# Windowed and pooled attention ahead of a gated feed-forward: from pair 12 on, every attention matmul becomes a 64x64 tile

## Chip, cores and metric

One Trainium2 chip, one of its cores. The metric is the device time in microseconds (us) of one execution, median of several; lower is better.

## The reference

Eight batches, eight heads, 576 positions, head dimension 64. Each head's attention is the sum of two parts. The first averages q, k and v over groups of four positions, attends among the 144 averages and repeats each result four times. The second lets every position see the positions less than four away. The result, as 4608 tokens by 512, goes through a feed-forward layer whose gate is a ReLU.

```python
q_d = q.reshape(B, H, Sd, factor, D).mean(axis=3)      # factor 4, Sd = 144; k_d, v_d alike
out_d = sm_attn(q_d, k_d, v_d)
out_up = np.repeat(out_d, factor, axis=2)
mask = np.abs(pos[:, None] - pos[None, :]) < factor
scores = np.where(mask, scale * np.matmul(q, k.transpose(0, 1, 3, 2)), -1e9)
out_local = np.matmul(softmax(scores), v)
x = (out_up + out_local).transpose(0, 2, 1, 3).reshape(B * S, H * D)
return (np.maximum(x @ w_gate, 0.0) * (x @ w_val)) @ w_out   # 512 -> 1536 -> 512
```

## The kernel before

**Pairs and chunks.** Two heads make a pair: head 0 lies on partitions 0 to 63, head 1 on 64 to 127. There are 32 pairs, four to a batch. The feed-forward works on chunks of 512 tokens, nine in all, each in two units of 256 tokens. Its result x, transposed, is the tile `xT`; `emit_h_mm` (L638) multiplies it with `w_gate` and `w_val`, ACT takes the ReLU (L647), DVE the product (L650), and the second product with `w_out` is done by a seven-product scheme on 128x256 quarters (`Unit.mm`, L723), whose sums are formed by DVE (L717). The last chunks use the same scheme for the first product too (L910).

**Order.** The schedule is by hand: the program emits each engine's instructions in the order of three token lists. `FRONT` covers pairs 0 to 11, `ORDER` is one period of four pairs and one chunk and is run for pairs 12 to 31, `TAIL` is what is left. A token is kind/argument/unit; within a period pairs a and b of units 0 and 1 follow each other. Each engine works through its own instructions in order.

**One pair's attention.** POOL issues the loads of q and k, cast to fp16 (L308), of v (`emit_load_v`, L333: 112 rows for each block of 96 queries, as the window reaches three further on either side) and of v grouped by four (`emit_load_v4`, L338). SP transposes q and k into `qkT` by DMA (L343); DVE sums groups of four into `qkd` (L350). POOL sums v by four in two steps (`emit_v2`, L385, and `emit_v1`, L391) into `vd`.

- `scores` (`emit_s1_mm`): pooled scores, four matmuls of 144 columns with 64 x 72 weights (L426); then for each of six blocks of 96 queries and both heads a matmul with 64 x 128 weights and 96 columns (L437). The two heads lie on the two row halves of PE. PSUM banks 4 to 7.
- `exp` (L447, twice) and `ed` (L461) on ACT, `mask` (L453, twice) on DVE.
- `o` (`emit_s2w_mm`), four times: three matmuls of 96 columns (L584) and two of 72 (L592) with weights 128 wide. Next to a head's 64 columns of v lie 64 columns of ones, so one matmul gives numerators on one half of the partitions and denominators on the other.
- `ln` (L602, twice, 64 partitions each) and `inv` (L607) on ACT give one over the denominator; `xn` (L611, twice, 64 partitions each) on DVE multiplies; `xsum` (L570) adds the pooled part, repeated four times, and writes `xT`.

Pairs 4 to 7 have another form, with denominators from a matmul with ones (`emit_den`, L527 and L536) and numerators apart (`emit_num`, L548 and L557), all 64 columns wide, so that the two heads lie on the two column halves. Pairs 8 to 11 have the `o` form, within `FRONT`.

**The start.** DVE sets tiles to constants, PE runs matmuls on a tile of zeros (`zero_sb`, L811), POOL issues the first loads of k and v. SP loads the first q and the constants and later issues the transposes and the output writes (L673), in the order of the program.

Of the kernel before, what the change touches and what calls it, by code (L numbers as in the profile page):

```python
# [106 lines left out]
"""  # L107
LATE = ("gate/5/1", "gate/4/1", "next/0/1", "next/1/1")
ORDER = """
p/1/0 gate/5/1< scores/a/0 keep/1/0 gate/4/1< hg/0/0 exp/a0/0 sumhi/0/0 sumhi/1/0 exp/a1/0  # L110
hv/0/0 mask/a0/0 ed/a/0 mask/a1/0 p/2/0 next/0/1< relu/0/0 next/1/1< o/a00/0 o/a01/0 c11//0
o/a10/0 ln/a0/0 o/a11/0 sum/2/0 p/6/0 v/a/1 sum/3/0 p/5/0 keep/2/0 pool/b/0 v2/b/0 ln/a1/0 p/7/0
hg/2/0 keep/3/0 after/3/0 v1/a/1 inv/a/0 c22//0 p/4/0 gate/0/0 v2/a/0 p/3/0 xn/a1/0 c21//0 relu/2/0 hg/1/0
xn/a0/0 qk/a0/1 hv/2/0 relu/1/0 qk/a1/1 c12//0 xsum/a/0 scores/b/0 qk/a2/1 next/0/0 hv/1/0
exp/b0/0 v/b/0 exp/b1/0 hg/4/0 mask/b0/0 gate/1/0 v4/a/1 ed/b/0 hg/3/0 mask/b1/0 relu/4/0
gate/2/0 v1/b/0 o/b00/0 o/b01/0 o/b10/0 pool/a/0 ln/b0/0 o/b11/0 hv/4/0 v2/a/1 ln/b1/0 hv/3/0
gate/4/0 inv/b/0 v4/b/1 next/1/0 p/1/1 relu/3/0 xn/b1/0 v4/b/0 p/2/1 keep/1/1 qk/a3/1 hg/5/0
xn/b0/0 qk/b0/1 p/6/1 gate/3/0 relu/5/0 qk/b1/1 scores/a/1 next/2/0 keep/2/1 next/3/0 hg/0/1
v/b/1 exp/a1/1 exp/a0/1 hv/5/0 mask/a1/1 qk/b2/1 ed/a/1 mask/a0/1 p/7/1 qk/b3/1 c11//1 gate/5/0
o/a00/1 keep/3/1 o/a01/1 o/a10/1 pool/b/1 ln/a0/1 o/a11/1 p/5/1 qk/a0/0> ln/a1/1 p/4/1 v/a/0>  # L120
c22//1 inv/a/1 hv/0/1 xsum/b/0 qk/a1/0> c21//1 xn/a0/1 p/3/1 relu/0/1 v2/b/1 hg/1/1 xn/a1/1
hg/2/1 relu/1/1 qk/a2/0> xsum/a/1 scores/b/1 c12//1 qk/a3/0> relu/2/1 gate/0/1 hg/3/1 exp/b1/1
v4/a/0> exp/b0/1 hv/1/1 mask/b1/1 ed/b/1 mask/b0/1 hv/2/1 gate/1/1 relu/3/1 pool/a/1 o/b00/1
o/b01/1 o/b10/1 ln/b0/1 o/b11/1 hv/3/1 qk/b0/0> gate/2/1 ln/b1/1 qk/b1/0> hg/5/1 gate/3/1
inv/b/1 v1/a/0> hv/4/1 relu/5/1 xn/b0/1 v1/b/1 hg/4/1 qk/b2/0> xn/b1/1 hv/5/1 relu/4/1 qk/b3/0>
xsum/b/1
"""


def _np_constants():  # L130
    i = np.arange(128)[:, None]
    p = np.arange(96)[None, :]
    band = ((i - p >= 0) & (i - p <= 6)).astype(np.float16)
    m_first = band * (i >= 3)
    m_last = band * (i <= 98)
    masks = np.stack([m_first, band, band, m_last], axis=1)
    pool = np.zeros((128, 176), np.float16)
    rw = np.arange(3, 99)
    pool[rw, 48 + (rw - 3) // 4] = 1.0
    t96 = np.arange(96)[:, None]  # L140
    eye = (t96 == np.arange(96)[None, :]).astype(np.float16)
    sum4 = (t96 // 4 == np.arange(24)[None, :]).astype(np.float16)
    t72 = np.arange(72)[:, None]
    rep4 = (t72 == np.arange(288)[None, :] // 4).astype(np.float16)
    cst = np.zeros((128, 384 + 176 + 120 + 288), np.float16)
    cst[:, 0:384] = masks.reshape(128, 384)
    cst[:, 384:560] = pool
    cst[:96, 560:656] = eye
    cst[:96, 656:680] = sum4
    cst[:72, 680:968] = rep4  # L150
    return cst


# [15 lines left out]
def kernel(  # L169
# [24 lines left out]
    LEAD = 4  # L194
    NTP = 9
    NVP = 11
    VS = 7
    NK = NJJ // 2
    B0 = 1
    WK = 112  # L200
# [5 lines left out]
    small = ctx.enter_context(tc.tile_pool(name="small", bufs=4))  # L206
    ypool = ctx.enter_context(tc.tile_pool(name="ypool", bufs=4))

    zero_sb = keep.tile([128, 640], FP16, name="zero_sb")
    cst_sb = keep.tile([128, 968], FP16, name="cst_sb")  # L210
    masks_sb = cst_sb[:, 0:384]
    pool_sb = cst_sb[:, 384:560]
    eye_sb = cst_sb[0:96, 560:656]
# [6 lines left out]
    def ring(n, shape, dtype, name):  # L220
        return [keep.tile(shape, dtype, name=f"{name}{i}") for i in range(n)]
# [3 lines left out]
    PS = 8  # L225
    qkfull = ring(NL, [128, 2, 2 * NB * 64], FP16, "qk16_")
    qk16 = [t[0:96] for t in qkfull]
    v4 = ring(NV4, [72, 4, 256], FP16, "v4_")
    v2full = ring(2, [128, 4, 128], FP32, "v2_")
    v2 = [t[0:72] for t in v2full]  # L230
    vwfull = ring(NL, [128, 2 * NB, 128], FP16, "vw_")
    vw = [t[0:WK] for t in vwfull]
    qkT = ring(4, [128, 2 * S + 32], FP16, "qkT_")
    qkd = ring(2, [128, 2, SD], FP16, "qkd_")
    ee = ring(2, [WK, 2, S + 32], FP16, "ee_")
    ed = ring(2, [72, 2, 2 * SD + 64], FP16, "ed_")
    vd = ring(3, [72, 2, 192], FP16, "vd_")
    xofull = keep.tile([128, 3, NB + 2, 128], FP16, name="xo")
    xo = [xofull[0:96, i] for i in range(3)]
    rden = keep.tile([128, 2, 360], FP32, name="rden")  # L240
# [4 lines left out]
    q32 = q32full[0:96]  # L245
    r1 = ring(3, [128, TCH], FP16, "r1_")
    gT = ring(2, [128, NJJ, TCH], FP16, "gT_")
    xT = keep.tile([128, NPB, NTOK], FP16, name="xT")
    ps = psum.tile([128, 8, 512], FP32, name="ps")

# [19 lines left out]
    nc.vector.memset(zero_sb, 0.0)  # L270
    nc.vector.memset(ones_sb[:, 0:64], 1.0)
    nc.vector.memset(ones_sb[:, 64:128], 4.0)
    for t in vw[0:4]:
        nc.vector.memset(t[:, :, 64:128], 1.0)
    for t in qkT:
# [15 lines left out]
    def head_off(hp):  # L291
        b = (hp // NPB + B0) % B
        return b, (b * H + 2 * (hp % NPB)) * S * D
# [17 lines left out]
        )  # L311

    def emit_load_v(hp):
        r = hp % NL
        b, off = head_off(hp)
        base = off - 3 * D
        t = vw[r][:, :, 0:64]
        n = 2 * NB
        if off == 0:
            nc.gpsimd.dma_start(  # L320
                t[:, 1:, :], _dap(v, base + NQ * D, [[D, WK], [NQ * D, n - 1], [1, D]])
            )
            nc.gpsimd.dma_start(t[3:WK, 0, :], _dap(v, 0, [[D, WK - 3], [1, D]]))
            nc.gpsimd.dma_start(t[0:3, 0, :], _dap(v, 0, [[D, 3], [1, D]]))
        elif b == B - 1 and hp % NPB == NPB - 1:
            nc.gpsimd.dma_start(
                t[:, 0 : n - 1, :], _dap(v, base, [[D, WK], [NQ * D, n - 1], [1, D]])
            )
            last = base + (n - 1) * NQ * D
            nc.gpsimd.dma_start(t[0:99, n - 1, :], _dap(v, last, [[D, 99], [1, D]]))  # L330
            nc.gpsimd.dma_start(t[99:WK, n - 1, :], _dap(v, last, [[D, WK - 99], [1, D]]))
        else:
            nc.gpsimd.dma_start(t, _dap(v, base, [[D, WK], [NQ * D, n], [1, D]]))  # L333

    def emit_load_v4(hp):
        b, off = head_off(hp)
        if hp >= NVP:
            nc.gpsimd.dma_start(  # L338
                v4[hp % NV4], _dap(v, off, [[4 * D, 72], [72 * 4 * D, 4], [1, 4 * D]])
            )  # L340

    def emit_qkT(hp):
        nc.sync.dma_start_transpose(  # L343
# [4 lines left out]
    def emit_pool(hp):  # L348
        with nc.allow_low_precision(reason="4:1 pooling sum"):
            nc.vector.tensor_reduce(  # L350
                out=qkd[hp % 2].rearrange("p i t -> p (i t)"),
                in_=qkT[hp % 4][:, 0 : 2 * S].rearrange("p (t f) -> p t f", f=4),
                axis=AX.X,
                op=ALU.add,
            )
# [14 lines left out]

    def emit_flipped(hp, i, pooled, eng, bank):
        if pooled:
            o = qkd[hp % 2].rearrange("p i t -> p (i t)").rearrange("p (b n t) -> p b n t", b=3, n=4)
        else:
            o = qkT[hp % 4][:, 0 : 2 * S].rearrange("p (b n t) -> p b n t", b=3, n=4)
        t = ps[:, bank, 0:480].rearrange("p (n t) -> p n t", n=4)
        copy_on(eng)(out=o[:, i], in_=t[:, :, 96:120] if pooled else t[:, :, 0:96])  # L377
# [2 lines left out]
        return nc.scalar.copy if eng == "A" else nc.vector.tensor_copy  # L380

    def emit_v2(hp):
        if NVP <= hp < NP:
            t, m = v4[hp % NV4], v2[hp % 2]
            nc.gpsimd.tensor_tensor(out=m, in0=t[:, :, 0:128], in1=t[:, :, 128:256], op=ALU.add)  # L385

    def emit_v1(hp):
        if not NVP <= hp < NP:
            return
        m, o = v2[hp % 2], vd[hp % 3]  # L390
        nc.gpsimd.tensor_tensor(  # L391
            out=o.rearrange("p c (x d) -> p x c d", x=3)[:, 0:3:2, :, :],
            in0=m[:, :, 0:64].rearrange("p (h c) d -> p h c d", h=2),
            in1=m[:, :, 64:128].rearrange("p (h c) d -> p h c d", h=2),
            op=ALU.add,
        )
# [180 lines left out]
    def emit_s2w_mm(hp, hh, g):  # L577
# [13 lines left out]
        for c in range(2):  # L591
# [4 lines left out]
                start=(c == 0),  # L596
                stop=(c == 1),
            )

    def emit_ln(hh):  # L600
        lo, de = 64 * hh, 64 - 64 * hh
# [406 lines left out]
    }  # L1008

    def scores(hp, a):  # L1010
        emit_s1_mm(hp, 4)
        if PS + 3 + LEAD <= hp + 3 < NP:
            emit_qkT(hp + 3)

# [3 lines left out]
    def pool_ab(hp, a):  # L1018
# [3 lines left out]

    PAIR_STEPS = {
        "scores": scores,
        "exp": lambda hp, a: emit_exp(hp, 4, int(a)),
        "mask": lambda hp, a: emit_mask(hp, int(a)),
        "ed": lambda hp, a: emit_ed(hp, 4),
        "o": lambda hp, a: emit_s2w_mm(hp, int(a[0]), int(a[1])),
        "ln": lambda hp, a: emit_ln(int(a)),
        "inv": lambda hp, a: emit_inv(),  # L1030
        "xn": lambda hp, a: emit_xnw(int(a)),
        "xsum": lambda hp, a: emit_xsum(hp),
        "pool": pool_ab,
        "v1": lambda hp, a: emit_v1(hp + 1),
        "v2": lambda hp, a: emit_v2(hp + 2),
# [66 lines left out]
    with tc.manual_schedule(engines={ET.PE, ET.DVE, ET.Activation, ET.SP, ET.Pool}):  # L1102
        nc.scalar.dma_start(cst_sb[0:96, 560:680], cst_dr[0:96, 560:680])
        emit_load_q1(0, 0)
        nc.sync.dma_start(cst_sb[:, 0:560], cst_dr[:, 0:560])
        nc.sync.dma_start(cst_sb[0:72, 680:968], cst_dr[0:72, 680:968])
        emit_warm(14, wide=True)
        for tok in FRONT.split():
            emit_front(tok)
# [37 lines left out]
```

## Time and profile before

| | |
|---|---|
| runs | 344.65, 345.5, 345.66 us; median 345.5 |
| profiled execution, first to last instruction | 343.5 us |
| what lies around the span (median less span) | 2.0 us |
| granted TensorE clock, mean | 0.998 |
| PE busy | 335.8 us (98%) |
| DVE, ACT, POOL busy | 295.2, 218.3, 181.9 us |
| L426 and L437, L584 and L592: matmuls | 128 and 384, 288 and 192 |

The profiled execution has no time of its own beside its span, so sums made from the trace are held against the span, and 2.0 us are added for the runs. Busy times of PE are modelled, and matmuls overlap: a row's mean for one matmul (203 ns for L437) is longer than the step from one to the next. What a stretch costs on PE is therefore read from the chain of work that ended last, in order of time, and from start times.

### The profile page before, as it was taken

To read this page: it belongs to the slowest core of one execution; us is meant where nothing else is said; L and a number is where in the kernel's file an instruction comes from. 1 tells how busy PE (TensorE), PEld (TensorE's weight loads), DVE (VectorE), ACT (ScalarE), POOL (GpSimd) and SP (SyncE) were. 2 spreads that over 40 slices of the span, in tenths; PEclk is the share of its full clock that TensorE was granted. 3 is DMA by queue.
4 is the path that set the end of the run, shared out by engine and by line. 5 is a ranking of instruction groups with operands and counts; after the bars stand their busy time and mean duration, and the time that the engine had idled before them with its cause. 6 is when DMAs were issued, how large, how long until landed. Compare 5 with 4: busy or idle time off the path is not lost.

```text
span 343.5 us, 8292 instructions
## 1 busy us (share of the span) xinstructions
PE 335.8 (98%) x3244; PEld 216.0 (63%) x3244; DVE 295.2 (86%) x546; ACT 218.3 (64%) x423; POOL 181.9 (53%) x232
## 2 busy tenths in 40 slices
PE   7899999999999999999999999999999999999996
PEld 3765556756575756575666656665766557768785
DVE  6695679988999999999999999999999798886892
ACT  3878766767767776676667767776677633334222
POOL 8986547776999893969297878740300000000000
PEclk9999999999999999999999999999999999999999
DMA  9999999999999999999989996991100001001023
GB/s 133 165 170 187 186 191 160 148 163 159 213 139 176 148 183 87 132 133 163 125 100 147 145 161 80 158 150 37 47 17 32 31 2 46 32 31 61 28 67 108
DMA packets 167882, 39.87 MB, mean 116 GB/s; under 512 B 149820, under 2 KB 164772, under 8 KB 167844
## 3 DMA queue, kind: packets, MB, share of 16 engines
q0 software_dynamic: 132160, 22.63, 92.1%
q1 hardware_dynamic: 35572, 16.71, 27.0%
q8 instruction: 25, 0.41, 0.5%
q14 instruction: 13, 0.11, 0.1%
q10 hardware_dynamic: 112, 0.02, 0.0%
HBM read 45.72 MB, written 9.44 MB: 161 GB/s over the span
## 4 chain that ended last, share of the span: by engine, by line
PE 90%; ACT 4%; DVE 3%; DMA 2%; issue 1%; POOL 0%; DVEq 0%; ACTq 0%; POOLq 0%
PE ps L638 48%; PE ps L723 23%; PE ps L910 4%; PE ps L584 4%; PE ps L437 2%; PE ps L426 2%; PE ps L592 2%; DMA vw<-in_v_dram 1%; PE ps L363 1%; PE ps L407 1%; DVE ee L453 1%; ACT qkT L377 1%; ACT ee L447 1%; ACT ed L461 1%; DVE xn L611 1%
## 5 line engine op out<-in xcount | busy, mean ns | idle before, releaser
L638 PE MATMUL ps<-xT,wv_sb 128*128 128x512 f16 x432 | 109.0, 379 | 0.0
L638 PE MATMUL ps<-xT,wg_sb 128*128 128x512 f16 x352 | 88.4, 380 | 0.0
L647 ACT ACTIVATE r<-ps 128x512 f16<-128x512 f32 x88 | 52.0, 596 | 31.6 <-PE ps L638 28.5
L638 PEld LDWEIGHTS <-wv_sb 128*128 128x128 f16 x432 | 40.4, 98 | 39.7
L650 DVE TENSOR_TENSOR gT<-r,ps 128x512 f16<-128x512 f16 x88 | 59.0, 680 | 6.7 <-PE ps L638 3.9
L638 PEld LDWEIGHTS <-wg_sb 128*128 128x128 f16 x352 | 32.6, 98 | 32.3 <-issue 0.2
L611 DVE TENSOR_TENSOR xn<-ps,rden 64x720 f16<-64x720 f32 x48 | 43.4, 905 | 5.3 <-ACT rden L607 4.1
L602 ACT ACTIVATE rden<-ps 64x720 f32<-64x720 f32 x48 | 36.7, 765 | 14.4 <-PE ps L592 13.3
L447 ACT ACTIVATE ee<-ps 112x576 f16<-112x576 f32 x64 | 38.8, 648 | 5.9 <-PE ps L437 4.9
L308 POOL DMA_DIRECT2D qk<-in_k_dram x46 | 33.9, 740 | 8.4 <-DMA qk<-in_q_dram 3.8
L308 POOL DMA_DIRECT2D qk<-in_q_dram x46 | 33.8, 740 | 6.9 <-DMA qk<-in_k_dram 1.7
L453 DVE TENSOR_TENSOR ee<-ee,cst_sb 112x576 f16<-112x576 f16 x64 | 32.3, 524 | 5.8 <-ACT ee L447 5.2
L723 PEld LDWEIGHTS <-gT 128*128 128x128 f16 x324 | 31.5, 98 | 9.0
L723 PEld LDWEIGHTS <-xo 128*128 128x128 f16 x288 | 27.4, 98 | 7.4
L333 POOL DMA_DIRECT2D vw<-in_v_dram x30 | 28.8, 960 | 5.8 <-PE ps L638 1.5
L350 DVE TENSOR_REDUCE qkd<-qkT 128x288 f16<-128x1152 f16 x23 | 30.9, 1344 | 0.0
L757 ACT COPY q<-ps 128x256 f32<-128x256 f32 x45 | 16.8, 373 | 21.1 <-PE ps L723 20.7
L723 PE MATMUL ps<-wo_sb,gT 128*128 128x256 f16 x216 | 28.0, 273 | 0.0
L723 PE MATMUL ps<-wt,xo 128*128 128x256 f16 x216 | 27.7, 272 | 0.0
L385 POOL TENSOR_TENSOR v<-v 72x512 f32<-72x512 f16 x21 | 24.8, 1182 | 3.7 <-DMA v<-in_v_dram 3.1
L920 ACT COPY vw<-ps 128x256 f32<-128x256 f32 x30 | 10.8, 374 | 20.7 <-PE ps L910 13.8
L570 DVE TENSOR_TENSOR xT<-xn 128x576 f16<-128x576 f16 x28 | 22.6, 808 | 0.5
(110 smaller groups left out, 556.9 us busy)
## 6 DMA issues: line engine op xcount, KB each, us to landing
out_dram<-y_sb SPq DMA_DIRECT2D x24, 256.0 KB, 4.0
vw<-in_v_dram POOLq DMA_DIRECT2D x30, 168.0 KB, 6.8
qk<-in_q_dram POOLq DMA_DIRECT2D x46, 72.0 KB, 6.6
qk<-in_k_dram POOLq DMA_DIRECT2D x46, 72.0 KB, 6.6
v<-in_v_dram POOLq DMA_DIRECT2D x21, 144.0 KB, 6.9
out_dram<-y_sb SPq DMA_DIRECT2D x22, 128.0 KB, 1.7
wg_sb<-in_moe_w_gate_dram POOLq DMA_DIRECT2D x4, 384.0 KB, 9.7
wv_sb<-in_moe_w_val_dram POOLq DMA_DIRECT2D x4, 384.0 KB, 10.5
```

The lines of the kernel that those rows point to most:

```text
L308: nc.gpsimd.dma_start(dst.rearrange("p (j h d) -> p j h d", h=2, d=64)[:, :, hh, :], _dap(src, off + hh * S * D, [[D, 96], [NQ * D, NB], [ ...
L333: nc.gpsimd.dma_start(t, _dap(v, base, [[D, WK], [NQ * D, n], [1, D]]))
L350: nc.vector.tensor_reduce(out=qkd[hp % 2].rearrange("p i t -> p (i t)"), in_=qkT[hp % 4][:, 0 : 2 * S].rearrange("p (t f) -> p t f", f=4), ...
L385: nc.gpsimd.tensor_tensor(out=m, in0=t[:, :, 0:128], in1=t[:, :, 128:256], op=ALU.add)
L447: nc.scalar.activation(out=o, in_=ps[0:WK, p0 + 2 * g : p0 + 2 * g + 2, 0:288], func=AF.Exp, scale=scale)
L453: nc.vector.tensor_tensor(out=o, in0=o, in1=_sap(masks_sb, (0, WK), 96 * g, [[0, 2], [1, 288]]), op=ALU.mult,)
L602: nc.scalar.activation(out=rden[lo : lo + 64], in_=ps[de : de + 64, 4 + 2 * hh : 6 + 2 * hh, 0:360], func=AF.Ln)
L611: nc.vector.tensor_tensor(out=xn[lo : lo + 64], in0=ps[lo : lo + 64, 4 + 2 * hh : 6 + 2 * hh, 0:360], in1=rden[lo : lo + 64], op=ALU.mult,)
L638: nc.tensor.matmul(out=out, lhsT=w[:, kk, bass.ts(jj, 128)], rhs=xT[:, kk, c * TCH : (c + 1) * TCH], start=(kk == 0), stop=(kk == 3),)
L647: nc.scalar.activation(out=r1[j % 3], in_=h1, func=AF.Relu)
L650: nc.vector.tensor_tensor(out=gT[c % 2][:, jj, :], in0=r1[j % 3], in1=h2, op=ALU.mult)
L723: nc.tensor.matmul(out=out, lhsT=left[:, i, :], rhs=right[i], start=(first and i == 0), stop=(i == NK - 1), skip_group_check=True,)
```

## The change

For pairs 12 to 31 the blocks of queries become 48 long. A block sees 54 keys, and 64 are taken. Even blocks lie on partitions 0 to 63 and odd ones on 64 to 127, for both heads, so that weights are 64 x 64 and four matmuls after one another go to four different quarters of PE.

- `emit_s1z`: pooled scores as 12 matmuls of 72 columns, windowed scores as 24 of 48; banks 4 and 5 only.
- `exp`, `mask` once for a pair, over 128 partitions x 576; `ed` 128 x 432.
- `den` (`emit_denz`): with ones as weights, 4 matmuls of 288 columns and 12 of 72 (three steps summed in PSUM), banks 6 and 7. `num` (`emit_numz`): 24 of 48 and 12 of 72, banks 4 and 5. On PE, `num` follows `den` with nothing between.
- `ln`, `xn` once for a pair, 128 x 720.
- v is loaded in two DMAs of 64 rows x 12 blocks (`emit_load_vz`). v by four is loaded in fp32 with two DMAs by SP instead of one with a cast by POOL; POOL's two sums work on 128 x 384 and 128 x 192; then two DMAs on SP copy the sums of each half of the partitions to the other, as both halves need both heads.
- Ahead of everything, POOL sets the three `v4` tiles (128 x 768 fp32) to zero; `near_sb`, the new mask, is one more load on SP; `zero_sb` is now part of `gT`.
- `ORDER` is the same list with the second tokens of `exp`, `mask`, `ln`, `xn` left out and the four `o` tokens replaced by `den` and `num`. `FRONT` and `TAIL` stay.

```diff
+    for t in v4:
+        nc.gpsimd.memset(t, 0.0)
...
     def emit_load_v4(hp):
+        if hp >= ZP:
+            t = v4[hp % NV4]
+            for h in range(2):
+                nc.sync.dma_start(
+                    t[64 * h : 64 * h + 48], _dap(v, off + h * S * D, [[4 * D, 48], [192 * D, 3], [1, 4 * D]])
+                )
...
+    def emit_load_vz(hp):
+        for par in range(2):
+            t = vz[hp % NL][64 * par : 64 * par + 64]
+            base = off + (48 * par - 3) * D
+                nc.gpsimd.dma_start(t, _dap(v, base, [[D, 64], [96 * D, 12], [1, D]]))
...
     def emit_v1(hp):
+        if hp >= ZP:
+            m, o = v2full[hp % 2], vdz[hp % 3]
+            nc.gpsimd.tensor_tensor(out=o[:, 0], in0=m[:, 0:3, 0:64], in1=m[:, 0:3, 64:128], op=ALU.add)
+            nc.sync.dma_start(o[64:112, 1], o[0:48, 0])
+            nc.sync.dma_start(o[0:48, 1], o[64:112, 0])
+            return
...
+    def emit_s1z(hp):
+        r4, f = hp % 4, qkdflat[hp % 2]
+        for c in range(3):
+            for g in range(2):
+                for h in range(2):
+                    rows, lo = slice(64 * h, 64 * h + 64), 288 + 72 * c
+                    nc.tensor.matmul(
+                        out=ps[64 * g : 64 * g + 64, 4 + h, lo : lo + 72].rearrange("p (j t) -> p j t", t=12),
+                        lhsT=f[rows, SD + 48 * c : SD + 48 * c + 64],
+                        rhs=f[rows, 0:SD].rearrange("p (j s t) -> p j s t", s=2, t=12)[:, :, g, :],
+                        start=True, stop=True)
+        t = qkT[r4]
+        for j in range(6):
+            for par in range(2):
+                for h in range(2):
+                    rows, lo = slice(64 * h, 64 * h + 64), 96 * j + 48 * par
+                    nc.tensor.matmul(
+                        out=ps[64 * par : 64 * par + 64, 4 + h, 48 * j : 48 * j + 48],
+                        lhsT=t[rows, S + lo - 3 : S + lo + 61],
+                        rhs=t[rows, lo : lo + 48],
+                        start=True, stop=True)
...
+    def emit_downz(hp, bank, left):
+        for c in range(3):
+            for g in range(2):
+                rows = slice(64 * g, 64 * g + 48)
+                for h in range(2):
+                    nc.tensor.matmul(
+                        out=ps[64 * h : 64 * h + 64, bank + g, 288:360],
+                        lhsT=left(rows, h ^ g, c),
+                        rhs=edfull[hp % 2][rows, h, 72 * c : 72 * c + 72],
+                        start=(c == 0), stop=(c == 2))
+
+    def emit_denz(hp):
+        for par in range(2):
+            rows = slice(64 * par, 64 * par + 64)
+            for h in range(2):
+                nc.tensor.matmul(
+                    out=ps[64 * h : 64 * h + 64, 6 + par, 0:288],
+                    lhsT=ones_sb[rows, 0:64],
+                    rhs=eefull[hp % 2][rows, h, 0:288],
+                    start=True, stop=True)
+        emit_downz(hp, 6, lambda rows, other, c: ones_sb[rows, 64:128])
+
+    def emit_numz(hp):
+        for j in range(6):
+            for par in range(2):
+                for h in range(2):
+                    nc.tensor.matmul(
+                        out=ps[64 * h : 64 * h + 64, 4 + par, 48 * j : 48 * j + 48],
+                        lhsT=t[rows, 6 * h + j, :],
+                        rhs=eefull[hp % 2][rows, h, 48 * j : 48 * j + 48],
+                        start=True, stop=True)
+        emit_downz(hp, 4, lambda rows, other, c: d[rows, other, c, :])
```

The first eighth of `ORDER`, after:

```
p/1/0 gate/5/1< scores/a/0 keep/1/0 gate/4/1< hg/0/0 exp/a/0 sumhi/0/0 sumhi/1/0 hv/0/0 mask/a/0
ed/a/0 p/2/0 next/0/1< relu/0/0 next/1/1< den/a/0 c11//0 ln/a/0 num/a/0 sum/2/0 p/6/0 v/a/1 sum/3/0
```

## Prediction

> **What bounds the kernel now.** I read the page first: the engines' shares and the chain that ended last.
>
> ```profile
> span 343.5 us, 8292 instructions
> ...
> PE 335.8 (98%) x3244; PEld 216.0 (63%) x3244; DVE 295.2 (86%) x546; ACT 218.3 (64%) x423; POOL 181.9 (53%) x232
> ...
> PE 90%; ACT 4%; DVE 3%; DMA 2%; issue 1%; POOL 0%; DVEq 0%; ACTq 0%; POOLq 0%
> ```
>
> PE is busy 98% and is 90% of the chain, so a change counts by what it does to PE's own stream; time taken off ACT and DVE counts only where PE waits for them. Next the chain in order of time (start, length, what) around one pair's attention:
>
> ```profile
> 67.72 2.59 PE ps L638 x12
> 70.31 0.18 PE ps L426 x2
> 70.49 0.13 PE ps L437 x6
> 70.62 0.06 PE ps L426 x2
> 70.68 0.13 PE ps L437 x6
> 70.81 2.70 PE ps L638 x12
> 73.50 0.13 PE ps L584 x3
> 73.64 0.07 PE ps L592 x2
> ```
>
> Two things are to be seen. The scores (L426, L437) are 0.50 us, and the twelve L638 matmuls behind them take 2.70 where the twelve before took 2.59. And one quarter of the outputs (L584, L592) is 0.20 us; the four quarters of a pair take 0.78 (64.76 to 65.54). The trace's start times say why. Matmuls 64 rows high on the two row halves start 3 ns apart and each such couple of 96 columns takes 42 ns, which is one matmul's streaming: they run side by side. Going from L638 to L426 costs 93 ns beyond the 216 ns that an L638 takes, and from L437 back to L638 92 ns beyond the 42; this repeats within 2 ns at every pair. I call these 0.185 us the price of one visit to small tiles. The outputs, full height and width, pay none. The pair's price on PE is 0.50 + 0.11 + 0.78 = 1.39 us.
>
> Side-by-side columns are shown by the first pairs, whose denominators and numerators are already 64 wide:
>
> ```profile
> 39.28 0.12 PE ps L527 x2
> 39.40 0.07 PE ps L536 x4
> 39.47 0.13 PE ps L548 x6
> ```
>
> Two 288-column matmuls in 0.12, four of 72 in 0.07: couples again, 0.033 us for 72 columns.
>
> Last, the start of the chain and the places where PE waits later:
>
> ```profile
> 0.64 0.66 issue
> 1.30 1.03 POOL qk L303
> 2.33 5.07 DMA vw<-in_v_dram
> ```
>
> ```profile
> 161.48 0.29 PE L584 MATMUL ps<-ee,vw 112*128 112x96 f16 x3 [0.35 <-DVE ee L453]
> ```
>
> The kernel starts with POOL issuing loads, and from pair 12 on one PE wait is worth naming: 0.51 us by start times before 161.48 (the other, 0.31 at 89.5, belongs to pair 11, which stays as it is).
>
> **PE, pairs 12 to 31 (20 pairs).** The new scores are 12 matmuls of 72 columns and 24 of 48, the denominators 4 of 288 and 12 of 72, the numerators 24 of 48 and 12 of 72, all on four 64x64 tiles in turn. If four run side by side, these are 3 + 6, 1 + 3 and 6 + 3 rounds. A 72-column round is 0.033 and a 288-column one 0.12 (rows above). No row has a 48-column round. From below: half of the 40 ns of a 96-column one and the same 2.5 ns beside it, 0.0225. From above: 0.033, since a 72-column round held its own 64-column weight loads. I take 0.028, near the shortest time from a 64-column weight load to its matmul in the start times (30 ns). Scores: 3 x 0.033 + 6 x 0.028 + one visit 0.185 = 0.45. Denominators and numerators follow each other on PE without a full-size matmul between, so they share one visit: 0.12 + 3 x 0.033 + 6 x 0.028 + 3 x 0.033 + 0.185 = 0.67. Sum 1.12 for 1.39: 0.27 less (0.20 to 0.33 by the two ends), times 20 is 5.4 us less (4.0 to 6.6).
>
> A rule is to be weighed here. The row: six L437 in 0.13 us, 22 ns each, couples 3 ns apart. The Trainium skill, TensorEngine Tiling (Array Packing), section Instruction Overhead, says that a matmul has about 60 cycles of overhead, that one column takes as long as 60, and that no tiling factor should come from a dimension that is already small; 48 columns are below it. Were that floor (25 ns, an estimate at the 2.4 GHz of its page on TensorE) paid by each instruction, the 88 matmuls would take 2.2 us and the time would be some 370 us, again an estimate; were it paid by each tile's round, the sum would gain 0.7 us. The row of couples speaks against the first reading.
>
> **ACT and DVE.** Rows of the costliest groups (busy us, mean ns, idle before):
>
> ```profile
> L611 DVE TENSOR_TENSOR xn<-ps,rden 64x720 f16<-64x720 f32 x48 | 43.4, 905 | 5.3 <-ACT rden L607 4.1
> L602 ACT ACTIVATE rden<-ps 64x720 f32<-64x720 f32 x48 | 36.7, 765 | 14.4 <-PE ps L592 13.3
> ```
>
> Each pair loses one of two exponentials (0.65), one Ln (0.77), one mask (0.52) and one product (0.91); ACT and DVE each lose 1.4 us per pair of about 9. PE covers all but the wait at 161.48: there the mask was late, it is now half the work, and I let 0.5 us go (0 to 0.5). Next late is nothing: between scores and denominators PE has two L638 groups and six L723, 2.4 us, for one exponential and one mask of 0.65 + 0.52.
>
> **The start.** Three POOL memsets of 128x768 fp32 now stand ahead of POOL's first load. The nearest row among POOL's groups:
>
> ```profile
> L1066 POOL MEMSET vw<- 112x768 f16 x3 | 2.5, 819 | 0.0
> ```
>
> It has as many elements per row in half the bytes; the instruction behind it starts 0.68 after it does. Three are 2.0 us from about 0.8 (DVE's first memset begins at 0.88), so the first load goes out near 2.9 to 3.1 instead of 1.30: 1.8 us late. From below 1.4 (the 0.66 of issue runs beneath them), from above 3.6 (twice the time for twice the bytes). The chain starts with just this load, and goes on through ACT and DVE without slack, so all of it is paid.
>
> **POOL, SP and DMA.** The v load becomes two issues (0.96 to about 2 x 0.8), the fp32 load (0.75) moves to SP, the two sums have fewer elements: POOL's total hardly moves. SP gains per pair two loads and two small copies that wait for POOL's sum; queued behind them are transposes and output writes. From pair 12 on the transposes go out 17 us or more before the pooling that reads them (73.5 and 90.4 for pair 12) and land in 7.8; POOL's sum ends 6 us or more before the matmul that reads it (92.9 and 98.9 for pair 12). The v loads have 1536 packets of 256 B for 1344, in a queue that runs as far ahead. I cost this at nothing; without that cover it is rival three.
>
> **Sum.** -5.4 - 0.5 + 1.8 = -4.1 us: span 339.4. The median of the runs (345.5) is 2.0 above the profiled span, so 341.4 us. The case's own ends: -6.6 - 0.5 + 1.4 and -4.0 + 3.6, 339.8 to 345.1.
>
> **Rivals.**
> *Only two tiles run at once* (slower). For it: no row shows row and column halves used together. Against: each alone runs as couples with nothing lost. Every round doubles: 2 x 0.756 + 0.37 = 1.88 per pair, +0.49 x 20 = +9.8; with the other terms 356.6 us. It decides from rounds 1.26 times my size on, where the 0.27 no longer pays for the start.
> *PE's sequencer can't feed it* (slower). 104 instructions, weight loads included, must pass in 0.49 us. The rows bound the rate from one side: after a semaphore wait at 19.60, 32 passed in 0.57 us, at most 18 ns each; the waits of L584 lie 0.45 to 1.2 us ahead of their matmuls, so the sequencer runs ahead. 104 x 18 ns less 1.0 of lead is 0.87, 0.38 more per pair, +7.6: 349.0 us. Should it be far faster, this is nothing.
> *SP's copies come late.* In pairs 14, 18, 22, 26 and 30 they go out behind a transpose (105.9 to about 113.7 for pair 14, needed at 117.1). A few us more of queueing stop PE; five stalls of 1 to 2 us, +7.5: 348.9 us.
> *Nothing is gained*: rounds at 0.033 and slow memsets leave it within 1 us.
>
> **How the numbers follow.** Forecast 0.60, two tiles 0.11, sequencer 0.10, copies 0.13, nothing 0.06. A measurement of this kernel can tell about 0.3%, 1.0 us. All of the forecast but its upper end (0.03) is faster: 0.57; same 0.09; slower 0.34. The range starts just below the forecast's own end and reaches up past the sequencer and the copies to 350; two tiles, and the far ends, stay out. The likeliest case alone is 339.8 to 345.1.
>
> **What would show it.** Right: scores in about 0.27 and denominators with numerators in about 0.49 us between full-size matmuls, four starts 3 ns apart, 93 ns at each change; no PE idle before either; first load near 3 us. Wrong: 48-column rounds at 0.05 or more (two tiles); matmuls that start singly 30 ns and more apart late in a burst (sequencer); PE idle released by vd or SP (copies); an L1066-like memset of 1.4 us (start).

## The result, and the profile after

The changed kernel takes 354.39 us (353.80 to 355.07); the kernel before, run beside it, 345.07. The ratio is 1.0265, with a 95% interval of 1.0232 to 1.0298. The forecast was 341.4 us, in a range from just below 339.8 to 350: wrong, and on the wrong side. The profiled execution, the shortest of the four, spans 351.9 us, 8.4 more than before. Times and ratios from here on leave out executions that took over 1.5% longer than the fastest of their kernel (one of the kernel without copies and early memsets, four of six with all sums on DVE, one of six with part of them there).

The page of the kernel after, its span, engines and chain:

```profile
span 351.9 us, 10404 instructions
...
PE 335.9 (95%) x4284; PEld 210.7 (60%) x4284; DVE 269.0 (76%) x508; ACT 191.9 (55%) x383; POOL 175.6 (50%) x235
...
PE 62%; DMA 20%; POOL 12%; issue 2%; SPq 2%; ACT 1%; DVE 0%; POOLq 0%; ACTq 0%
```

DVE and ACT did become 26 us less busy each, as the change says. But PE's share of the chain fell from 90% to 62%, and DMA (2% before), POOL (none) and SP's queue now stand in it. The waits of the kernel after name the DMA (engine, line, what it waited for; us in total, times, longest):

```profile
PEld L700 <- DMA vd<-vd: 7.2, 6, 2.0
...
PE ps L700 <- DMA vd<-vd: 6.5, 6, 1.9
...
PE ps L640 <- DVE ee L509: 1.9, 1, 1.9
```

The first two rows are the same waits, once for the weight load and once for its matmul; the third is pair 11, whose mask (L509) comes late. `vd<-vd` are the two small copies that take POOL's pooled v from one half of the partitions to the other; L700 are the 72-column matmuls that close denominators and numerators. One such wait, pair 14, in three timelines of the kernel after: POOL, then SP, then PE.

```profile
113.71 0.62 POOL L442 TENSOR_TENSOR vd<-v 128x192 f16<-128x192 f32 x1
```

```profile
115.72 0.54 SPq L443 DMA_DIRECT2D vd<-vd  x1
116.30 0.59 SPq L444 DMA_DIRECT2D vd<-vd  x1
117.40 3.65 SPq L363 DMA_DIRECT2D v<-in_v_dram  x4
```

```profile
121.27 0.35 PE L727 MATMUL ps<-ee,vw 64*64 64x48 f16 x24
121.45 0.20 PE L700 MATMUL ps<-ed,vd 48*64 48x72 f16 x1
123.53 0.29 PE L700 MATMUL ps<-ed,vd 48*64 48x72 f16 x11 [1.88 <-DMA vd<-vd]
```

POOL's sum ends at 114.3. SP is still issuing the two loads of v by four (113.67 to 115.6), then issues the copies, 1.2 us. Their first packet moves at 120.06, 3 us after the second issue, and PE goes on at 123.5, 9.2 us after the sum. PE wanted it at 121.45: the sum stood 7.1 us ahead, and PE waits 2.05 by start times. The page's DMA issues give the landing (KB each, median us from issue):

```profile
vd<-vd SPq DMA_DIRECT2D x40, 18.0 KB, 6.2
qkT<-qk SPq DMA_TRANSPOSE x23, 8.4
```

18 KB take about as long as everything else that waits its turn there; the page's row of DMA shares has a 9, the highest digit, in each of its first 27 slices of 40.

**Where the 8.4 us are**, by PE's start times from 58 us on, counting waits over 0.18 us (medians for the pair):

| | before | after | difference |
|---|---|---|---|
| start, up to the first 256-column matmul | 58.29 | 59.23 | +0.9 |
| one pair on PE (scores + denominators + numerators) x 20 | 1.38 | 0.50 + 0.76 | -2.4 |
| waits for the copies (pairs 12, 14, 16, 18, 20, 26) | 0 | 7.5 | +7.5 |
| pair 15's wait, for which the profile names no releaser | 0 | 0.8 | +0.8 |
| pair 11's wait for its mask | 0.31 | 2.05 | +1.7 |
| the wait near 161 | 0.51 | 0 | -0.5 |

The sum is +8.0 of 8.4.

### The profile page after: what moved, and what is told of

Read it like the earlier page. It is cut to its first block, busy times and chain, and to the rows that moved or that the text cites. A ratio compares the mean times of both kernels' runs of the same rounds, so it can differ in the third digit from the quotient of the medians.

```text
span 351.9 us, 10404 instructions
## 1 busy us (share of the span) xinstructions
PE 335.9 (95%) x4284; PEld 210.7 (60%) x4284; DVE 269.0 (76%) x508; ACT 191.9 (55%) x383; POOL 175.6 (50%) x235
## 4 chain that ended last, share of the span: by engine, by line
PE 62%; DMA 20%; POOL 12%; issue 2%; SPq 2%; ACT 1%; DVE 0%; POOLq 0%; ACTq 0%
PE ps L786 32%; PE ps L871 16%; DMA qk<-in_k_dram 8%; DMA vw<-in_v_dram 4%; DMA vd<-vd 4%; PE ps L1058 4%; POOL vw L385 3%; POOL qk L324 3%; DMA wv_sb<-in_moe_w_val_dram 3%; POOL v L430 2%; POOL qk L319 2%; PE ps L408 1%; POOL vw L352 1%; POOL vd L442 1%; PE ps L463 1%
## 5 line engine op out<-in xcount | busy, mean ns | idle before, releaser
L430 POOL TENSOR_TENSOR v<-v 128x384 f32<-128x384 f32 x20 | 21.6, 1079 | 15.7 <-DMA v<-in_v_dram 15.2
L737 ACT ACTIVATE rden<-ps 128x720 f32<-128x720 f32 x20 | 15.4, 770 | 15.8 <-PE ps L700 15.5
L687 DVE TENSOR_TENSOR ee<-ee,near_sb 128x576 f16<-128x576 f16 x20 | 10.1, 503 | 17.7 <-ACT ee L683 17.5
L755 ACT ACTIVATE rden<-rden 128x720 f32<-128x720 f32 x28 | 22.5, 804 | 0.7
L622 DVE TENSOR_TENSOR xn<-ps,rden 128x720 f16<-128x720 f32 x24 | 21.7, 903 | 1.5 <-ACT vd L472 0.6
L1077 DVE TENSOR_TENSOR xT<-ps,vw 128x256 f32<-128x256 f32 x30 | 12.5, 421 | 8.7 <-ACT vw L1068 4.0
```

The source lines that it names most:

```text
L430: nc.gpsimd.tensor_tensor(out=v2full[hp % 2][:, 0:3, :], in0=t[:, :, 0:128], in1=t[:, :, 128:256], op=ALU.add)
L622: nc.vector.tensor_tensor(out=xn, in0=ps[:, num : num + 2, 0:360], in1=rden, op=ALU.mult)
L737: nc.scalar.activation(out=rden, in_=ps[:, 6:8, 0:360], func=AF.Ln)
L755: nc.scalar.activation(out=rden, in_=rden, func=AF.Exp, scale=-1.0)
```

## The experiments

### The copies left out

The two copies are gone and the other half's pooled sums are a constant.

```diff
-            nc.sync.dma_start(o[64:112, 1], o[0:48, 0])
-            nc.sync.dma_start(o[0:48, 1], o[64:112, 0])
```

> The changed kernel without the two copies between partition halves; the other half's pooled sums are a constant, so that part of the output is left out. Copies theory (PE waits 8.3 us in seven pairs because the two copies land some 7 us after POOL's sum): those waits go, 354.4 - 8.3 = 346 us; the 2.1 us wait of pair 11 stays. Load theory (more DMA traffic makes POOL late, and the copies are only the last link): PE then waits for POOL's sum itself, at most 3 us are gained, 351 us or more.

Measured: 349.59 us, ratio 1.0102 (1.0043 to 1.0162), span 346.6. The waits for `vd<-vd`, 7.5 us, are gone, and the span falls by 5.3. Waits of 0.38 and 0.56 us near 112 us for DVE are new, pair 15's grew from 0.85 to 2.32 us, and pair 11's 1.99 stays. The copies are the larger part of the loss, not all of it.

Pair 15's wait, here and in the kernel after, is not for a copy: there its copies are issued from 108.64 to 110.00 and the second lands 3.8 us after its issue, some 20 us early. PE stops between the ninth and the tenth of twelve matmuls, in the kernel after (timeline, PE) as well as here and in the kernel without any sum further down:

```profile
131.95 0.27 PE L700 MATMUL ps<-ed,vd 48*64 48x72 f16 x9
132.89 0.22 PE L700 MATMUL ps<-ed,vd 48*64 48x72 f16 x3 [0.67 <-issue]
```

"issue" means that no releaser is to be seen. The page lists a DMA queue that loads instructions; before, then after (packets, MB, share):

```profile
q8 instruction: 25, 0.41, 0.5%
```

```profile
q8 instruction: 33, 0.54, 0.7%
```

Its packets are 16 KB, and there is one for each 260 of PE's weight loads and matmuls (6524 before, 8584 after). Numbered from 0 in order of start, the instructions that end the ten waits put down to "issue" from 58 us on, in nine kernels of this document, all leave 193 over when divided by 256; those that end waits with a named releaser do not. Each wait ends 1.2 to 2.0 us after such a packet does. Before, from 68 us on, the packet ends 7 us or more ahead of that instruction, after the change often 2 to 6. So PE waits for its own instructions, of which the new form has more; place and time show this, no run changed it.

### The copies on ACT's queue

`nc.sync` becomes `nc.scalar` for both copies: nothing of SP's stands before them.

> The same two copies, issued by ACT instead of SP. If the copies are late because they stand in SP's queue behind transposes and v loads, they land in 2 to 3 us and PE's waits for them go: 346 to 348 us, with some cost on ACT, which has 45% to spare. If they are late because the DMA engines themselves are full, landing stays at 6 us or more and the time within 1.5 us of 354.4.

Measured: 366.51 us, ratio 1.0568 (1.0499 to 1.0636). The landing, from the DMA issues of this kernel:

```profile
vd<-vd ACTq DMA_DIRECT2D x40, 18.0 KB, 6.5
```

6.5 us from a queue that holds nothing else by then, against 6.2 from SP's: the order on SP is not what makes a landing slow. What fits is that the time passes behind the loads in the DMA engines: copies issued where those are quiet (after some 235 us) move their first packet within 1 us. And ACT now stands still until POOL's sum is there, so that its ReLUs and copies out of PSUM come late. ACT's next work behind two copies that follow a sum (POOL ends it at 109.56, ACT issues the first copy at 109.59):

```profile
110.81 0.80 ACT L755 ACTIVATE rden<-rden 128x720 f32<-128x720 f32 x1 [3.12 <-POOL v L430]
```

The waits of PE in this kernel:

```profile
PE ps L700 <- DMA vd<-vd: 6.1, 3, 2.5
PE ps L871 <- ACT r L795: 3.3, 2, 2.7
PE ps L786 <- ACT y_sb L916: 3.3, 4, 2.5
```

### The memsets later, with and without the copies

POOL's three memsets move from ahead of the first load to a place some 50 us on.

```diff
-    for t in v4:
-        nc.gpsimd.memset(t, 0.0)
...
-... den/7/1/5 flip/9 ev/8/11V/2 ...
+... den/7/1/5 flip/9 zero ev/8/11V/2 ...
```

> The three POOL memsets moved from the start to near 50 us. Start theory: the first load goes out 1.5 us earlier and the 0.9 us that the stage up to 60 us lost is back: 353.4 us. If POOL's lateness of 1.5 us is also what makes pair 11's sum (2.1 us of PE wait) and the later sums late, 2 to 4 us are back: 350.5 to 352.5 us.

> Both: memsets late, and no copies (the other half's pooled part is left out). If PE then waits for nothing, what is left is the change of PE's own stream: per pair 0.76 + 0.50 us by start times in the changed kernel against 1.38, 20 x 0.115 = 2.3 us, and the two waits of the kernel before, 0.8 us: 345.1 - 3.1 = 342 us. If pair 11's wait stays, 344 us. If DMA traffic holds it, 348 us or more.

Measured: with the copies 354.62 us, 1.0275 (1.0219 to 1.0331), no gain to be seen; without them 348.59, 1.0055 (1.0019 to 1.0091). The first 256-column matmul starts at 58.29 before. It starts at 59.05 to 59.54 in four traces with early memsets (the kernel after at 59.23) and at 58.77 to 59.07 in six with late ones; in two more with late ones, where PE had 3.4 us of half clock from 12 us on, at 60.2 and 60.4. So the memsets are worth some 0.4 us there. The rest of the 0.94 was not taken apart. Without copies and early memsets PE still waits 3.5 us: 1.02 for a mask at 73.6, 2.23 at 135.5 for POOL's sum itself (`vd` by POOL, no DMA between), and 0.27 at 231.1 at a place where it needs new instructions (number 193 over 256, as above). The sum is made too late even for a matmul that needs no copy.

### Matmuls alone

A kernel that holds only matmuls on constants (and writes zeros as output): twelve rounds in a row of four 64x64 tiles, of couples 64 columns of weights wide, of couples 64 rows high, and of one tile, each with 16 to 96 columns, with 128x128 matmuls of 256 columns between.

> Matmuls alone, no attention (its output is zeros): 12 rounds of four 64x64 tiles with new weights for each matmul, 16 to 96 columns, couples of column halves and of row halves likewise, and one tile by itself. If a round of four is held up by passing eight instructions (about 4 ns each), quads stay at 32 ns up to 72 columns and couples fall to 16. If by a tile's own 64-column weight load, couples and the single tile stop falling near 30 ns too. If by neither, quads of 48 columns take 22.5 ns and the 32 of the kernel come from what surrounds them.

Measured, step from one round to the next, mean of the last eight:

| columns | four 64x64 tiles | two, 64-wide weights | two, 128-wide weights, 64 rows | one 64x64 tile |
|---|---|---|---|---|
| 16 to 48 | 31.6 to 31.8 ns | 31.6 | 25.0 | 31.6 |
| 64 | 31.6 | 31.8 | 29.1 | |
| 72 | 32.5 | 32.5 | 32.5 | 32.5 |
| 96 | 42.5 | 42.5 | 42.5 | 42.5 |

From its groups, by form (busy us, mean ns; the counts include the single tile's twelve where it had these columns):

```profile
L34 PE MATMUL ps<-x,w 64*64 64x96 f16 x60 | 1.4, 205 | 0.0
...
L34 PE MATMUL ps<-x,w 64*64 64x72 f16 x60 | 1.2, 197 | 0.0
L34 PE MATMUL ps<-x,w 64*64 64x48 f16 x60 | 1.1, 188 | 0.0
L34 PE MATMUL ps<-x,w 64*64 64x16 f16 x60 | 1.1, 174 | 0.0
```

Four tiles cost what one costs, so all four run side by side. But a round of 16 columns costs what one of 64 does, and the floor of 31.6 ns belongs to one tile alone: not the passing of instructions, which one tile would pay a quarter of. It falls to 25.0 where the weights are 128 wide, so it goes with the shape of the weights. What fits, though no run shows it by itself, is that a tile can't begin its next matmul before its own next weights are in. The first round of a burst takes some 52 ns. The Trainium skill, TensorE: Matmul & The Clock Gate, section LDWEIGHTS, gives a load one nanosecond for each 1.2 columns of weights; that would be 53 ns for 64 columns, an estimate by that page. The rows here do not agree: a whole round with new weights takes 31.6.

### The sums earlier, the memsets where they were, and later

Only the order on POOL: of the two pairs of a unit the one needed first is summed first, and its second sum directly follows.

```diff
-... v2/b/0 ... v1/a/1 ... v2/a/0 ... v1/b/0 den/b/0 ... v2/a/1 ... v2/b/1 ... v1/a/0> ... v1/b/1 ...
+... v2/a/0 ... v1/b/0 ... v2/b/0 ... v1/a/1 den/b/0 ... v2/a/1 v1/b/1 ... v2/b/1 v1/a/0> ...
```

> The changed kernel with the order of POOL's sums altered, nothing else: the sum of the pair that is needed first goes first, and a pair's second sum directly behind its first, so that the copies go out 5 to 20 us earlier. If the copies' 6 us are the cause and lead is the cure, PE's 8.3 us of waits for them go as in the run without copies: 347 to 349 us, ratio 1.01. If POOL has no room to be earlier, the waits move to POOL's sum and 352 us or more remain.

> The same with the three memsets moved to near 50 us as well. If both delays are gone, the ratio to the kernel before is 0.995 to 1.005 (PE's stream is 2.3 us shorter, the waits that POOL's sums cause are left); if the memsets are worth only what the start lost, 0.5 us below the run without that move.

Measured: 347.16, ratio 1.0030 (1.0006 to 1.0054); with the memsets late as well 345.27, ratio 0.9981 (0.9956 to 1.0006). No arithmetic is gone, and nearly the whole loss is. The copies land no faster (median 6.1 us); they are issued early enough: pair 14's first one at 110.86 instead of 115.72. The late memsets are worth 1.9 us here, where 0.5 was expected; pair 11's wait for its mask is 2.72 us in the first trace, at 90.3, and 0.49 in the second. In the first, 0.7 us after that wait, PE runs at half its clock (two windows: length, then busy time of PE, its weight loads, DVE, ACT and POOL with the instructions, then the granted clock, DMA share and GB/s):

```profile
90.00:94.00 4.00, 1.45 (x23) 0.92 (x21) 4.00 (x4) 0.83 (x3) 4.00 (x6) 0.98 1.38 163
94.00:97.00 3.00, 3.00 (x12) 1.14 (x10) 1.82 (x3) 2.19 (x3) 3.00 (x5) 0.50 1.10 157
```

From 93.9 to 97.3 the 512-column matmuls start 427 ns apart instead of 216: a wait of 2.7 us cost about 1.5 us more.

### POOL's sums left out

The late memsets, no copies, and from pair 11 on no sums on POOL either; the pooled part of v is a constant.

> POOL's sums of v by four and the copies are left out from pair 11 on (the pooled part uses a constant), memsets late. In the run without copies a mask on DVE took 2.3 us instead of 0.5 while POOL summed beside it. If DVE and POOL hinder each other, then without POOL's sums every mask takes about 0.5, PE's remaining 3.4 us of waits go and the span is 341 us (ratio 0.995). If it is the DMA load, the waits stay and the span is 344 us or more.

Measured: 343.42 us, ratio 0.9918 (0.9888 to 0.9948), span 341.6, waits 0.67 us in all (pair 15's, at "issue"). The masks tell why pair 11 waited. One row each of the kernel before, of the kernel after and of this one (ns: shortest, median, longest):

```profile
L453 DVE TENSOR_TENSOR ee<-ee,cst_sb x64: 444/456/1267, 11.2 to 266.7; 112x576 f16<-112x576 f16 x64
```

```profile
L509 DVE TENSOR_TENSOR ee<-ee,cst_sb x24: 445/451/2391, 12.1 to 91.3; 112x576 f16<-112x576 f16 x24
L687 DVE TENSOR_TENSOR ee<-ee,near_sb x20: 451/459/1035, 100.1 to 274.6; 128x576 f16<-128x576 f16 x20
```

```profile
L504 DVE TENSOR_TENSOR ee<-ee,cst_sb x24: 444/451/459, 11.8 to 89.1; 112x576 f16<-112x576 f16 x24
L682 DVE TENSOR_TENSOR ee<-ee,near_sb x20: 451/459/460, 97.7 to 264.4; 128x576 f16<-128x576 f16 x20
```

The same instruction takes 0.45 us or up to 2.4; without sums on POOL none takes more than 0.46. Sums are not the whole of it: of eleven masks over 0.6 us in the kernel before, four (0.74 to 0.98) have only DMA issues of POOL beside them by the start times, and why those are long stays open. Where the longest happened, in the timeline of the kernel without copies:

```profile
89.13 3.49 DVE L507 TENSOR_TENSOR ee<-ee,cst_sb 112x576 f16<-112x576 f16 x2
89.44 1.01 POOL L430 TENSOR_TENSOR v<-v 128x384 f32<-128x384 f32 x1
90.40 0.73 POOL L445 TENSOR_TENSOR vd<-v 72x256 f16<-72x256 f32 x1
91.21 1.10 POOL L430 TENSOR_TENSOR v<-v 128x384 f32<-128x384 f32 x1
...
92.77 0.29 PE L638 MATMUL ps<-ee,vw 112*128 112x96 f16 x3 [1.82 <-DVE ee L507]
```

Two masks, 0.9 us of work, take 3.49 beside three sums. The Trainium skill, SBUF — State Buffer, section SBUF: two separate sides, says that DVE and GpSimd share a pair of ports, that a DVE operation with two inputs in SBUF needs it when GpSimd reads SBUF too, and that who starts first keeps it for the whole instruction. That they get in each other's way is what these rows show; that the first one keeps it is not: by the start times the first mask begins 0.31 us ahead of the first sum, and it still lasts 2.3 us.

### The sums on DVE

If POOL's sums harm DVE, DVE could make them: `nc.gpsimd` becomes `nc.vector` in both sums, on top of the early sums and late memsets, for pairs 12 to 31 and, in a second kernel, for 16 to 31.

> The order with the sums of v early, the memsets late, and both sums of v by four for pairs 12 to 31 on DVE instead of POOL. Theory (POOL's sums stretch DVE's masks, and the copies only need their sums early): POOL's 1.0 + 0.6 us per pair become about 0.45 + 0.26 us on DVE (384 and 192 elements in fp32 at about one element in 1.1 ns, the step of DVE's mask would give more), DVE has 1.4 us per pair free, no mask beside a sum is above 0.6 us any more, and the time falls from 345.3 towards the 343.4 of the kernel without sums: 343.5 to 344.5. Rival (DVE in order, waiting for a load of v by four of 144 KB that lands late, or full in the front, where it is busy 93% from 60 to 120 us): DVE's masks of pairs 11 to 14 come late, PE waits 1 to 3 us there, and the time is 346 or more.

> As the kernel with the sums on DVE, but only from pair 16 on; the sums of pairs 12 to 15, which fall where DVE is fullest, stay on POOL. Theory: masks from about 125 us on are all near 0.46 us, the waits at 75 and 92 us stay as they are on POOL (0.5 to 1 us each), 344 to 345. Rival (DVE blocked by late loads): as slow as or slower than with the sums on POOL, 346 or more, with PE waits for DVE after 125 us.

Measured: 358.00, ratio 1.0347 (1.0300 to 1.0394), and 359.55, ratio 1.0368 (1.0331 to 1.0405). The rival held, and for far more than the 346 that it named as its least. On DVE the sums are short (0.55 and 0.36 us), and the longest mask is 0.46 us in both kernels (in the second POOL still makes the sums up to pair 15, but none falls beside a mask). But once in each period of four pairs DVE stands waiting for the load of v by four. The timeline of the second kernel, DVE, and two windows of it, in the columns as above (PE idle, then its clock at half):

```profile
132.53 0.56 DVE L428 TENSOR_TENSOR v<-v 128x384 f32<-128x384 f32 x1 [8.30 <-DMA v<-in_v_dram]
```

```profile
127.00:131.00 4.00, 0.30 (x2) 0.02 (x1) 0.00 (x0) 0.52 (x2) 1.95 (x4) 1.00 1.68 166
131.00:134.00 3.00, 0.00 (x0) 0.00 (x0) 1.43 (x3) 0.00 (x0) 1.87 (x3) 0.56 1.56 118
```

POOL's sums waited for loads of v by four too. From the waits of the kernel after:

```profile
POOL v L430 <- DMA v<-in_v_dram: 15.2, 4, 10.8
```

POOL's own time has room for that; its 50% busy shows how much. On DVE the whole feed-forward stands behind it.

### That load earlier

The load (pairs 17, 21, 25, 29) is issued right behind the sum that frees its buffer; once with DVE's sums from pair 16 on, once with POOL's.

```diff
-v2/b/0 p/3/0 ...    and    ... xn/b/0 v4/b/0 p/2/1 ...
+v2/b/0 v4/b/0 p/3/0 ...    and    ... xn/b/0 p/2/1 ...
```

> As the kernel with the sums on DVE from pair 16 on, and of each period the load of v by four that DVE waited for (pairs 17, 21, 25, 29; issued near 124 us, landed at 132.5, wanted at 124.2) issued some 10 us earlier on SP, behind the sum that frees its buffer. Theory (the 360 us came from that one load alone): DVE's waits of 16.4 us for it go, no PE wait above 1 us stays behind 115 us, masks are near 0.46 us, and the time is 343.5 to 345. Rival (DVE has no room for 0.55 + 0.36 us more per pair, or the clock's drops after the waits weigh more than the waits): 347 or more with PE waiting for DVE elsewhere.

> The order with the sums of v early and the memsets late, sums on POOL, and the same load of v by four issued earlier. Theory (POOL has room, so its 14.6 us of waiting for that load cost nothing, and what is left are masks beside POOL's sums): the same as without the earlier load, 344.5 to 346. Rival (POOL's wait put its sums beside DVE's masks or held back loads): 343.5 to 344.5.

Measured: 346.45, ratio 1.0001 (0.9975 to 1.0026), and 346.47, ratio 1.0008 (0.9980 to 1.0037). With DVE's sums the 16.4 us of waiting are gone and so are 13 us of time: that load was the cause. The gain on top of it that I expected is not there. Waits of 1.29 us at 90.3 and 1.5 us between 110 and 115 remain, where POOL still makes the sums up to pair 15 (a mask at 108.6 took 1.93 us), and one of 0.97 at 155.3, one of the ten for new instructions. With POOL's sums the earlier load changes nothing, as expected.

No version that computes the whole beats the kernel before by more than the interval; early sums with late memsets (0.9981) come to the same time.

## Why the prediction was wrong

**The step that failed** is the sentence on POOL, SP and DMA that ends "I cost this at nothing". It held a cover of "6 us or more" between POOL's sum and the matmul against nothing: the landing time was never set beside it, though the rows for it were there (6.6 us for a load, 7.8 for a transpose, in full DMA engines). The sum, for pair 14, is 1.4 us until SP comes to the copies, 1.2 for two issues, 6.6 to land and release PE: 9.2 against 7.1 of cover. That is +7.5 us in six pairs where nothing stood, and it is rival three, which was given 0.13. That the rival's price was +7.5 as well is luck: I put it at pairs 14, 18, 22, 26 and 30, behind a transpose on SP's queue; it is 12, 14, 16, 18, 20 and 26, pair 14's copies stood behind loads of v, and ACT's queue gives the same landing. The rest of the miss is below: 341.4 + 7.5 for the copies + 3.0 for PE's stream + 1.7 for pair 11 + 0.8 for instructions - 0.9 at the start is 353.5, beside 353.8 for the profiled execution.

**PE's stream** went the way that was said and a good half less far. The timeline of the kernel after, PE, at pair 12's scores:

```profile
98.56 0.29 PE L662 MATMUL ps<-qkd 64*64 64x72 f16 x12
98.68 0.36 PE L674 MATMUL ps<-qkT 64*64 64x48 f16 x24
98.97 1.04 PE L786 MATMUL ps<-xT,wg_sb 128*128 128x512 f16 x4
```

From the first small matmul to the next full one are 0.41 us, and the 93 ns of the change into small tiles lie ahead of that: 0.50, where 0.45 was forecast. Denominators and numerators, here at pair 13, which waits for nothing:

```profile
112.80 0.32 PE L712 MATMUL ps<-ee,ones_sb 64*64 64x288 f16 x4
...
113.47 1.47 PE L786 MATMUL ps<-xT,wv_sb 128*128 128x512 f16 x6
```

0.67 and 0.093 again make 0.76 where 0.67 was forecast, together 2.4 us saved instead of 5.4. Four tiles do run at once (starts 3 to 4 ns apart, 93 ns at each change into them), so the two-tile rival is not in the time. Nor is the sequencer's, as it was put; that the instructions themselves come late was in no term (+0.8). Three terms of PE's sum were mis-sized, and the start times give each its share of the 0.14 us per pair (medians of 20 pairs). The twelve 48-column rounds, taken at 0.028, are 0.032, the upper end of my bounds: 0.05. The first round of each visit is 0.053 where 0.033 was taken, and 0.147 where 0.12 was: 0.05. The change back behind the numerators is 0.13 where 0.092 was taken: 0.04; why it is longer than the 0.094 of matmuls alone at 72 columns stays open. Cutting 96 columns to 48 could not halve a round: with new 64-column weights it stays at 32 ns.

**The start.** The chain of the kernel after, at its beginning:

```profile
0.74 2.09 POOL v L286 x3
2.83 0.97 POOL qk L319
```

Three memsets are 2.09 us, as said (2.0), and the first load goes out at 2.83 instead of 1.30. "All of it is paid" was wrong: 1.53 us late, of which some 0.4 is paid at 59 us, going by the traces with late memsets; the 0.94 of the table holds more than the memsets.

**The wait at 161.48** went, 0.5 us, as said. Its reason, "the mask was late", was half of it: the kernel before has masks of up to 1.27 us beside POOL's sums. "Next late is nothing" did not look at that. Pair 11's wait "stays as it is" became 2.05 us, since POOL's sums for pairs 12 and 13 now run beside its masks.

## What to carry to other kernels

A small copy that an engine will wait for costs its place in the issuing queue, the issues and a landing under the load of that moment; set that sum beside the slack before calling it hidden, and if it is larger, make what it copies earlier. Before cutting matmuls into smaller tiles, measure one tile's round with its own weight load: from 64 columns down to 16 nothing was saved here. Smaller tiles also mean more instructions, and these are loaded by the same busy DMA engines. An engine with slack may wait for a late load for nothing; the same work on an engine without it brings the wait into the time.

## What the runs showed of the hardware that I had not expected

A 64x64 tile takes a new weight load and matmul every 31.6 ns at best, whatever its columns up to 64, and four tiles do so at once; with 128-wide weights it is 25.0. A DVE multiplication of two SBUF tiles stretches from 0.45 to as much as 2.51 us beside POOL's sums (in the kernel with early sums), and to no more than 0.46 when these are left out or all on DVE. A copy of 18 KB within SBUF lands 6.2 to 6.5 us after its issue beside full DMA engines, from SP's queue or ACT's alike. A PE wait of 2.7 us was followed by 3.4 us of half clock; with the copies on ACT's queue one of 2.2 us was too, and three of 2.6 to 2.8 us were not. PE's instructions come in packets of 16 KB, one for each 260, and PE stood still for 0.3 to 2.3 us where one came late.
